# Last outputs in halves of heads with the gate behind them, a second search level on rounded 16-bit places, and another order of the first turn of x

## The chip, the cores and the metric

The kernel runs on one core of one Trainium2 chip. The metric is the time of one execution on the device in microseconds (us). Its engines are PE (TensorE; PEld is its weight load), DVE (VectorE), ACT (ScalarE), POOL (GpSimd, which issues the gathers and scatters) and SP (SyncE, which issues plain transfers).

## What is computed

A retention layer gives x, and a mixture of eight experts is applied to it. B=4, H=8, S=768, D=64; N=3072 tokens, DM=512, E=8 experts with F=1024, and a capacity of N/E=384 tokens each.

```
for t in range(S):
    state = gamma * state + einsum('bhd,bhe->bhde', k[:, :, t], v[:, :, t])
    y[:, :, t] = scale * einsum('bhd,bhde->bhe', q[:, :, t], state)
x = y.transpose(0, 2, 1, 3).reshape(N, DM)
logits = x @ w_gate                                  # [N, E]
for idx in argsort(-logits.flatten()):               # greedy, best first
    tok, e = idx // E, idx % E
    if assigned[tok] < 0 and counts[e] < N // E:
        assigned[tok] = e; counts[e] += 1
for e in range(E):
    out[assigned == e] = relu(x[assigned == e] @ w1[e]) @ w2[e]
```

Every product with a weight is made of three: a number is split into a high part (w1h, w2h, xh, hh) and a rest (w1l, w2l, xlo, hl), and high by high, high by rest and rest by high are summed.

## The kernel before

**Retention.** The 4 batches by 6 chunks of 128 tokens are 24 units, in 14 groups of one or two. For a group, `scores` makes masked scores (am, on DVE), `outputs` starts y from the state (T by queries, into the PSUM tile yp), `mix` adds the values by am and ACT copies yp to ys, and `states` goes on. `gate(c)` multiplies ys of chunk c by the gate's weights (32 matmuls), ACT copies the logits (gs), and PE transposes them. Behind the last group come eight `by_two` matmuls over the chunks that are already known, the last gate, the transpose, and four more `by_two`. The rows of x that are left are transposed in between (xr) and written to DRAM (xs) by SP.

**Search.** For each expert in turn the threshold of its 384 best tokens is sought in levels of 64 candidates: `cmp` compares the 24 tokens of each of the 128 partitions with 64 thresholds th (128x1536 results, in two instructions), PE counts them (x12 matmuls), DVE negates half of the counts (ng) and makes of them which expert is full (sg), PE adds over partitions, and DVE takes the place of the step (nmb). The second level takes its 64 thresholds inside the step that was found. Then come the threshold tv, the full expert's code, the chosen tokens Wq, their running places (Sc, s) and, by a one-hot of the places (A, V, ob), the token numbers idx, by which POOL gathers x (xg). bad, et, oix, eo and lim close an expert, and m, oh, eqc, a open the next. The first expert's search stands alone; the others stand between the experts' matmuls.

**Turn and experts.** A gathered tile of 128 tokens is transposed by PE (`turn_x`, L1029, pt), copied by ACT (xh, L1034) and subtracted by DVE (xlo). Three tiles make an expert's 384 tokens. Then `mm1` runs f0 to f7, twelve products each (L1079), ACT takes the positive part (hh) and DVE its rest (hl), and `mm2` runs three tiles of 24 products (L1121), whose results ACT copies (yo) and POOL scatters. For the first expert `by_thirds` (L1058) makes the products of w1h by xh of f0 and f1 as each third of x comes in, so that `mm1` has only the products with w1l and with xlo left for these two; `HOT` (23) and `WAIT` (3) are matmuls on zeros that fill PE's time ahead of the first tile and behind the first turn.

**Order.** Each engine runs its instructions in the order in which the code issues them. For the experts a planner in the code does this: it adds up a clock for PE, DVE, POOL and DMA (DVE by the number of elements of each counted instruction), and after each three products decides whether a step of the next search (`side.tick`), a split of weights, a gather or a turn is issued (`feed.tick`). What an expert needs and isn't issued when it begins is issued there at once (`force`). All counted DVE instructions carry the line of a helper: L162 before, L165 after.

Of the kernel before, what the change touches and what calls it, by code (L numbers as in the profile page):

```python
# [56 lines left out]
WAIT = 3  # L57
THIRDS = 2
FILL = (5, 7)
READY0 = 0  # L60
BITS = (6, 6, 5, 5, 5, 5)
# [4 lines left out]
def tile_retention_moe(ctx: ExitStack, tc: tile.TileContext, qkv, wg, w1, w2,  # L66
# [26 lines left out]
    near = sw.tile([128, 4], F32, name="near")  # L93
    top = sw.tile([128, 1], F32, name="top")
    gridn = [sw.tile([128, 64], F32, name=f"gridn{i}") for i in range(2)]
# [21 lines left out]
    def constants():  # L117
# [6 lines left out]
        nc.gpsimd.iota(iot, pattern=[[1, 64]], base=0, channel_multiplier=0, allow_small_or_imprecise_dtypes=True)  # L124
        for t, k in ((iolow, 1), (iohigh, 32)):
            nc.gpsimd.iota(t, pattern=[[k, t.shape[1]], [0, t.shape[2]]], base=0, channel_multiplier=0,
                           allow_small_or_imprecise_dtypes=True)
# [109 lines left out]
    def span_parts(pool, psum):  # L237
# [19 lines left out]
        def grids():  # L257
# [8 lines left out]
            for i, f in enumerate((WINDOW / 64, WINDOW / 4096, -WINDOW, -WINDOW * 65 / 64)):  # L266
                nc.vector.tensor_scalar(near[:, i:i + 1], step, float(f), None, op0=OP.mult)
            for i in range(2):
                nc.vector.tensor_scalar(gridn[i], iot, near[:, i:i + 1], near[:, i + 2:i + 3], op0=OP.mult, op1=OP.add)
# [7 lines left out]
    offn, qn = {}, {}  # L277
# [120 lines left out]
    def outputs(us):  # L398

        c = units[us[0]][1]  # L400
        for u in us:
            yps[u] = rp.tile([128, HP, C], F32, name="yp", bufs=2)
        if c:
            for pr in range(HP):
                for u in us:
                    b = units[u][0]
                    for s in range(2):
                        o = 64 * (s ^ b % 2)
                        nc.tensor.matmul(yps[u][o:o + 64, pr, :], T[b // 2][64 * s:64 * s + 64, b % 2, pr, :],  # L409
                                         st[u][1][64 * s:64 * s + 64, pr, :], start=(pr == 0), stop=False,  # L410
                                         skip_group_check=True)
# [4 lines left out]
    def mix(us):  # L416

        c = units[us[0]][1]
        for u in us:
            b, yp = units[u][0], yps.pop(u)  # L420
            for pr in range(HP):
                for s in range(2):
                    o = 64 * (s ^ b % 2)
# [993 lines left out]
```

## Time and profile before

| | |
|---|---|
| time, median of 3 runs | 403.05 us (403.01 to 403.31) |
| profiled execution | 400.03 us, its span 398.3 us |
| PE busy | 387.9 us, 97% of the span |
| DVE, ACT, POOL busy | 68%, 39%, 37% |
| retention ends, first search | 82.5 to 97.9 us |
| first turn of x | 102.2 to 110.4 us |
| PE's last matmul ends | 392.9 us |

The profile is of one execution. A row of the timeline is: start, duration, engine, line, operation, out<-in, partitions x elements and type, count, and in brackets how long the engine was idle before it and what ended that. Instructions that stand together are one row with a count. Behind PE's last matmul come the last copies and the last scatter, up to 398.3.

### The profile page before, as it was taken

The page shows a single profiled execution, that of the slowest core. Times are in us where ns is not written, and L with a number is a line of the kernel's source. Part 1 is how long each engine was busy: PE and PEld are TensorE (multiplying, and loading weights), DVE is VectorE, ACT ScalarE, POOL GpSimd, SP SyncE. Part 2 cuts the span into 40 slices and gives each one's busy share as a digit, 9 for nine tenths or more (in the row PEclk, how much of TensorE's full clock was granted, in tenths as well). Part 3 has the DMA queues.
Part 4 walks back from the last instruction along what each step waited for, and adds up shares of the span by engine and source line. Part 5 has one row for each costly group of instructions (what it writes and reads, how often), then busy time and mean ns, then how long its engine had stood idle before and what let it go on. Part 6 is the DMA issues. An engine that isn't in the chain of part 4 may idle for free.

```text
span 398.3 us, 8481 instructions
## 1 busy us (share of the span) xinstructions
PE 387.9 (97%) x3460; PEld 338.6 (85%) x3462; DVE 269.9 (68%) x641; ACT 156.4 (39%) x285; POOL 148.0 (37%) x165
## 2 busy tenths in 40 slices
PE   8999999998999999999999999999999999999994
PEld 6988989974798889879988987898799889889983
DVE  6459868967998589858868885887687157156300
ACT  1422424243471265147325524343454165156210
POOL 6488783202520720361262341353265138021011
PEclk9999999999999999999999999999999999999999
DMA  7999988987653671483365482366147316710001
GB/s 291 423 414 420 408 312 259 227 209 257 198 199 105 183 256 54 143 289 135 107 212 238 149 294 112 95 221 241 54 160 251 144 53 183 318 54 26 2 27 59
DMA packets 22824, 77.50 MB, mean 195 GB/s; under 512 B 2677, under 2 KB 11639, under 8 KB 16121
## 3 DMA queue, kind: packets, MB, share of 16 engines
q0 software_dynamic: 8448, 46.14, 33.0%
q1 hardware_dynamic: 14330, 30.74, 21.5%
q8 instruction: 29, 0.48, 0.5%
q14 instruction: 17, 0.14, 0.1%
HBM read 64.29 MB, written 12.58 MB: 193 GB/s over the span
## 4 chain that ended last, share of the span: by engine, by line
PE 68%; issue 13%; DVE 7%; DMA 7%; POOL 2%; ACT 1%; POOLq 1%; SPq 0%; another core or an unknown queue 0%; DVEq 0%; ACTq 0%
PE py L1121 25%; PE ph L1079 24%; DMA ld<-qkv 5%; PE yp L424 4%; PE sc L377 3%; PE pt L1029 2%; PE psm L162 2%; PE yp L409 2%; DVE am L380 2%; PE sc L514 1%; PE TP L439 1%; DVE cmp L162 1%; DMA out<-yo,oix 1%; POOL wraw L983 1%; DMA xg<-xs,idx 1%
## 5 line engine op out<-in xcount | busy, mean ns | idle before, releaser
L1079 PE MATMUL ph<-xh,w1h 128*128 128x384 f32 x248 | 81.8, 343 | 0.0
L1079 PE MATMUL ph<-xlo,w1h 128*128 128x384 f32 x256 | 81.7, 335 | 0.0
L1079 PE MATMUL ph<-xh,w1l 128*128 128x384 f32 x256 | 81.5, 335 | 0.0
L1121 PE MATMUL py<-w2h,hh 128*128 128x512 f32 x184 | 75.2, 409 | 0.0
L1121 PE MATMUL py<-w2l,hh 128*128 128x512 f32 x184 | 72.1, 392 | 0.0
L1121 PE MATMUL py<-w2h,hl 128*128 128x512 f32 x184 | 72.1, 392 | 0.0
L1102 POOL DMA_INDIRECT out<-yo,oix x23 | 27.9, 1215 | 106.1 <-ACT yo L1099 99.4
L983 POOL DMA_INDIRECT wraw<-w,wix x32 | 38.5, 1203 | 60.8 <-DVE un L162 47.0
L1084 ACT ACTIVATE hh<-ph 128x384 fp32r<-128x384 f32 x64 | 31.4, 490 | 62.0 <-PE ph L1079 61.3
L162 DVE TENSOR_TENSOR w1l<-wraw,w1h 128x1024 fp32r<-128x1024 f32 (+1 forms) x36 | 39.2, 1101 | 14.2 <-ACT w1h L1002 14.2
L1079 PEld LDWEIGHTS ph<-xlo,w1h 128*128 128x128 f32 x256 | 47.7, 188 | 0.0
L1079 PEld LDWEIGHTS ph<-xh,w1l 128*128 128x128 f32 x256 | 47.7, 188 | 0.0
L1079 PEld LDWEIGHTS ph<-xh,w1h 128*128 128x128 f32 x248 | 46.4, 188 | 1.1 <-ACT xh L1034 0.4
L162 DVE SCALAR_TENSOR_TENSOR hl<-ph,hh 128x384 fp32r<-128x384 f32 x64 | 34.8, 553 | 18.2 <-ACT hh L1084 17.7
L1016 POOL DMA_INDIRECT xg<-xs,idx x24 | 28.7, 1196 | 41.3 <-issue 30.9
L380 DVE TENSOR_TENSOR am<-sc,dm 128x512 f32<-128x512 f32 x48 | 30.0, 683 | 18.4 <-PE sc L377 18.4
L1121 PEld LDWEIGHTS py<-w2h,hl 128*128 128x128 f32 x184 | 34.5, 188 | 7.4
L162 DVE TENSOR_TENSOR w2l<-wraw,w2h 128x1024 fp32r<-128x1024 f32 x32 | 38.6, 1219 | 2.3 <-ACT w2h L1002 2.3
L1121 PEld LDWEIGHTS py<-w2l,hh 128*128 128x128 f32 x184 | 34.7, 189 | 6.2 <-DVE w2l L162 0.6
L1121 PEld LDWEIGHTS py<-w2h,hh 128*128 128x128 f32 x184 | 34.7, 188 | 5.6
L1099 ACT ACTIVATE yo<-py 128x512 f32<-128x512 f32 x23 | 13.7, 597 | 58.6 <-PE py L1121 43.3
L1002 ACT ACTIVATE w1h<-wraw 128x1024 fp32r<-128x1024 f32 (+1 forms) x36 | 33.6, 957 | 4.7 <-DMA wraw<-w,wix 4.7
(189 smaller groups left out, 556.0 us busy)
## 6 DMA issues: line engine op xcount, KB each, us to landing
ld<-qkv SPq DMA_DIRECT2D x20, 1024.0 KB, 11.9
xs<-x SPq DMA_DIRECT2D x32, 128.0 KB, 3.4
ld<-qkv SPq DMA_DIRECT2D x4, 768.0 KB, 5.3
xs<-xr SPq DMA_DIRECT2D x7, 256.0 KB, 2.2
wraw<-w,wix POOLq DMA_INDIRECT x32, 7.3
xg<-xs,idx POOLq DMA_INDIRECT x24, 3.7
out<-yo,oix POOLq DMA_INDIRECT x23, 3.1
xs<-x SPq DMA_DIRECT2D x4, 64.0 KB, 1.8
```

Of the source, the lines that this page charges most:

```text
L162: return f(o, *a, **k)
L377: nc.tensor.matmul(sc[s][:, pr, :], k_[r, w], q_[r, w], start=True, stop=True)
L380: masked.append(nc.vector.tensor_tensor(am[:, s], sc[s], dm[:, s], op=OP.mult))
L424: nc.tensor.matmul(yp[o:o + 64, pr, :], values(u)[:, 2 * pr + s, :], st[u][0][:, s, pr, :], start=(not c and pr == 0), stop=(pr == HP - 1) ...
L983: nc.gpsimd.indirect_dma_start(out=t, out_offset=None, in_=w1v if nm == "w1" else w2v, in_offset=bass.IndirectOffsetOnAxis(ap=wix[:, hf:hf ...
L1002: nc.scalar.activation(p[0], p[2], AF.Copy)
L1016: nc.gpsimd.indirect_dma_start(out=t, out_offset=None, in_=xs, in_offset=bass.IndirectOffsetOnAxis(ap=found[n][0][:, j:j + 1], axis=0))
L1079: nc.tensor.matmul(ph, a[:, o:o + 128], x_[:, d], start=(k == 0 and not begun), stop=(k == len(prods) - 1), skip_group_check=begun)
L1084: nc.scalar.activation(hh[:, f], ph, AF.Relu)
L1099: nc.scalar.activation(yo, py, AF.Copy)
L1102: sct = nc.gpsimd.indirect_dma_start(out=out, out_offset=bass.IndirectOffsetOnAxis(ap=oix[:, j:j + 1], axis=0), in_=yo, in_offset=None, bo ...
L1121: nc.tensor.matmul(py, h_[:, f, t], a[:, o:o + DM], start=(k == 0), stop=(k == 23))
```

## The change

1. In the last group (`halved`) `outputs` and `mix` work in two halves of the heads, each in a PSUM bank of its own, and ACT copies four halves of 128x256. `gate(NC - 1)` stands directly behind the loop; the eight early `by_two` come behind it and end their sum, ng is taken from it at once, and the last two chunks are counted in eight matmuls of 64x8.
2. In the second level of the search the 64 thresholds are no longer compared. From the step's start (`starts`, `at`, two columns) each token's place in the grid, x, is worked out, rounded to a whole number in 16 bits (`place`, four copies) and compared with the numbers 0 to 63 (`ramp`). `off`, `qn`, `q` and `sel` go; tv comes first, `ge` is new.
3. In the first turn of x one filling matmul stands behind the first turn (`WAIT`), the second turn comes next, then both thirds of the first tile, and so on; the search's step stands ahead of the rest of the weights and of xlo.

```diff
-WAIT = 3
+WAIT = 1
...
+NEAREST = 12582912.0
...
     def below(n, tv):
         th = sw.tile([128, 64], F32, name="th")
-        ve.tensor_scalar(th, gridn[0], tv, None, op0=OP.add)
+        ve.tensor_scalar(th, gridn, tv, None, op0=OP.add)
         yield th
-        offn[n] = sw.tile([128, 64], F32, name="off")
-        ve.tensor_scalar(offn[n], gridn[1], tv, None, op0=OP.add)
-        qn[n] = sw.tile([128, 1], F32, name="qn")
-        ve.tensor_scalar(qn[n], gridn[1][:, 0:1], tv, near[:, 1:2], op0=OP.add, op1=OP.subtract)
+        starts[n] = sw.tile([128, 2], F32, name="starts")
+        ve.tensor_scalar(starts[n], near[:, 3:5], tv, None, op0=OP.add)
         yield
+
+    def places_in_grid(m, at):
+        x = sw.tile([128, COLS], F32, name="x")
+        ve.tensor_scalar(x, m, at, near[:, 5:6], op0=OP.subtract, op1=OP.mult)
+        place = sw.tile([128, COLS, 4], BF, name="place")
+        ve.tensor_scalar(place, bc(x, 4), NEAREST, -NEAREST, op0=OP.add, op1=OP.add)
+        return place
+
+    def reach_place(cols, place, cmp):
+        p_ = place[:, cols]
+        k = p_.shape[1]
+        tt(cmp[:, cols].rearrange("p c (j r) -> p c j r", r=4), p_[:, :, None, :].to_broadcast([128, k, 16, 4]),
+           ramp.rearrange("p (j r) -> p j r", r=4)[:, None].to_broadcast([128, k, 16, 4]), OP.is_ge)
...
-            for u in us:
-                mix([u])
-                states([u])
+            if g == len(groups) - 1:
+                mix(us)
+            else:
+                for u in us:
+                    mix([u])
+                    states([u])
...
+        gate(NC - 1)
         pc = rp.tile([128, 2 * E], F32, name="sc", bufs=4)
...
-            by_two(pc, cmp0, oh0, c, k == 0, False)
+            by_two(pc, cmp0, oh0, c, k == 0, k == len(early) - 1)
...
-        gate(c)
-        next(rows)
         lt = rp.tile([128, 512], F32, name="sc", bufs=4)
         nc.tensor.transpose(lt[:, 0:128], gs[c % 2], ident)
+        n0 = other_half(pc, nc.vector)
...
-        for b in range(B):
-            by_two(pc, cmp0, oh0, b * NC + NC - 2, False, b == B - 1)
-        n0 = other_half(pc, nc.vector)
+        for k in (NC - 2, c):
+            for b in range(B):
+                te.matmul(pc[0:64, 0:E], cmp0[:, b * NC + k, :], oh0[:, b * NC + k, :], start=False, stop=True,
+                          skip_group_check=True)
...
                 if not i:
-                    th = sw.tile([128, 64], F32, name="th")
-                    ve.scalar_tensor_tensor(th, nm.to_broadcast([128, 64]), near[:, 0:1], offn[n], op0=OP.mult,
+                    at = sw.tile([128, 2], F32, name="at", bufs=2)
+                    ve.scalar_tensor_tensor(at, nm.to_broadcast([128, 2]), near[:, 0:1], starts[n], op0=OP.mult,
                                             op1=OP.add)
                     cmp = sw.tile([128, COLS, 64], BF, name="cmp", bufs=2)
+                    place = places_in_grid(m, at[:, 1:2])
                     for h in range(2):
-                        cc = slice(h * COLS // 2, (h + 1) * COLS // 2)
-                        reach(cc, COLS // 2, m, cmp, th)
+                        reach_place(slice(h * COLS // 2, (h + 1) * COLS // 2), place, cmp)
                         if not h and n:
                             yield
-                    q = sw.tile([128, 1], F32, name="q", bufs=2)
-                    ve.scalar_tensor_tensor(q, nm, near[:, 0:1], qn[n], op0=OP.mult, op1=OP.add)
                 else:
+                    tv = sw.tile([128, 1], F32, name="tv", bufs=2)
+                    ve.scalar_tensor_tensor(tv, nm, near[:, 2:3], at[:, 0:1], op0=OP.mult, op1=OP.add)
                     eh = sw.tile([128, E], BF, name="eh")
                     ve.scalar_tensor_tensor(eh, num, nm, codet, op0=OP.is_equal, op1=OP.mult)
-                    tv = sw.tile([128, 1], F32, name="tv", bufs=2)
-                    ve.scalar_tensor_tensor(tv, nm, near[:, 1:2], q, op0=OP.mult, op1=OP.add)
+                    ge = sw.tile([128, COLS], BF, name="ge")
+                    ve.tensor_scalar(ge, m, tv, None, op0=OP.is_ge)
                     ve.tensor_reduce(code, eh, axis=AX.X, op=OP.max)
-            sel = sw.tile([128, COLS], BF, name="sel")
-            ve.tensor_scalar(sel, a, code, None, op0=OP.is_equal)
-            ve.scalar_tensor_tensor(Wq[:, 0:COLS], m, tv, sel, op0=OP.is_ge, op1=OP.mult)
+            ve.scalar_tensor_tensor(Wq[:, 0:COLS], a, code, ge, op0=OP.is_equal, op1=OP.mult)
...
     lows = []
+    turn_x(0, 0, lows)
+    fill(WAIT)
     for j in range(KT):
-        if j == 1:
-            by_thirds(0, range(1))
-        turn_x(0, j, lows)
-        if not j:
-            fill(WAIT)
-        if j:
-            side.step()
-            by_thirds(j - 1, range(1 if j == 1 else 0, THIRDS))
-        if j < KT - 1:
+        if j + 1 < KT:
+            turn_x(0, j + 1, lows)
+        by_thirds(j, range(THIRDS))
+        side.step()
+        if j + 1 < KT:
             low_w(quarters[j])
         lows.pop(0)[1]()
-    by_thirds(KT - 1, range(THIRDS))
-    side.step()
```

The order on DVE in the first turn of x, before. w1l is the rest of the weights of f0 and f1, xlo that of x, ng and sg belong to the first level's counts of expert 1:

```order
L162 TENSOR_TENSOR cmp<-m,th 128x768
L162 TENSOR_TENSOR w1l_1802<-wraw_98,w1h_1801 128x512
L162 TENSOR_TENSOR xlo<-pt,xh 128x4x128
L162 TENSOR_SCALAR ng<-psm 64x8
L162 TENSOR_TENSOR w1l_1802<-wraw_98,w1h_1801 128x512
L162 TENSOR_TENSOR xlo<-pt,xh 128x4x128
L162 SCALAR_TENSOR_TENSOR sg_93<-psm,ng 64x8
L162 TENSOR_TENSOR xlo<-py,xh 128x2x128 x2
L162 TENSOR_REDUCE nmb<-psm 128x1
L162 SCALAR_TENSOR_TENSOR th<-nmb,near,off 128x64
L162 TENSOR_TENSOR cmp<-m,th 128x768
```

The same stretch after:

```order
L165 TENSOR_SCALAR ng<-psm 64x8
L165 TENSOR_TENSOR w1l_1810<-wraw_98,w1h_1809 128x512
L165 TENSOR_TENSOR xlo<-pt,xh 128x4x128
L165 SCALAR_TENSOR_TENSOR sg_93<-psm,ng 64x8
L165 TENSOR_TENSOR w1l_1810<-wraw_98,w1h_1809 128x512
L165 TENSOR_TENSOR xlo<-pt,xh 128x4x128
L165 TENSOR_REDUCE nmb<-psm 128x1
L165 SCALAR_TENSOR_TENSOR at<-nmb,near,starts 128x2
L165 TENSOR_SCALAR x<-m,at,near 128x24
L165 TENSOR_SCALAR place<-x 128x96
L165 TENSOR_TENSOR cmp<-place,ramp 128x768
L165 TENSOR_TENSOR xlo<-py,xh 128x2x128 x2
```

ng went from behind the first xlo to ahead of the first w1l, and the last xlo (x2) from ahead of nmb to behind the comparison.

DVE around the first part of w2l of expert 0 (two instructions for one half of the weights), before: un ends the search of expert 1, s to bad number its tokens.

```order
L162 TENSOR_TENSOR un<-un,Wq 128x24
L162 TENSOR_TENSOR w2l_1971<-wraw,w2h_1970 128x1024 x2
L162 SCALAR_TENSOR_TENSOR hl<-ph,hh 128x384
L162 SCALAR_TENSOR_TENSOR s_2035<-psm,Wq 128x24
L162 SCALAR_TENSOR_TENSOR bad<-psm,bad 128x1
```

The end of the same block after:

```order
L165 SCALAR_TENSOR_TENSOR bad<-both,code,bad 128x1
L165 TENSOR_REDUCE et<-oh 128x1
L165 TENSOR_REDUCE et<-un 128x1
L165 SCALAR_TENSOR_TENSOR bad<-et,bad 128x1
L165 SCALAR_TENSOR_TENSOR hl<-ph,hh 128x384 x2
L165 TENSOR_TENSOR w2l_1995<-wraw,w2h_1994 128x1024
L165 TENSOR_TENSOR w2l_2048<-wraw,w2h_2047 128x1024 x2
```

One of the two stays ahead of s; the second stands behind the block and two hl, directly ahead of the other half of the weights.

PE at the third turn of expert 1 (pt), where mm2 of expert 0 (py) ends and f0 of expert 1 (ph) begins, before:

```order
L1029 MATMUL pt<-ident,xg 128x128 x4
L1121 MATMUL py<-w2h_2013,hh 128x512
L1121 MATMUL py<-w2l_2014,hh 128x512
L1121 MATMUL py<-w2h_2013,hl 128x512
L1121 MATMUL py<-w2h_2013,hh 128x512
L1121 MATMUL py<-w2l_2014,hh 128x512
L1121 MATMUL py<-w2h_2013,hl 128x512
L1079 MATMUL ph<-xh,w1h_2229 128x384 x3
```

And after:

```order
L1056 MATMUL pt<-ident,xg 128x128 x4
L1148 MATMUL py<-w2h_2047,hh 128x512
L1148 MATMUL py<-w2l_2048,hh 128x512
L1148 MATMUL py<-w2h_2047,hl 128x512
L1056 MATMUL pt<-ident,xg 128x128 x4
L1106 MATMUL ph<-xh,w1h_2216 128x384 x3
```

No product of mm2 stands between the turn and the first product with xh any more. At expert 3 the third turn also stands directly ahead of the first product.

## Rows read from the trace of the kernel before

**Rows 1.** The page: busy us, share of the span and instructions of each engine.

```profile
PE 387.9 (97%) x3460; PEld 338.6 (85%) x3462; DVE 269.9 (68%) x641; ACT 156.4 (39%) x285; POOL 148.0 (37%) x165
```

**Rows 2.** Stretches: us, busy PE PEld DVE ACT POOL, clock, DMA share, GB/s.

```profile
82.50:97.90 15.40, 12.81 (x152) 8.82 (x150) 10.65 (x48) 6.11 (x15) 1.26 (x3) 1.00 0.79 228
107.60:393.00 285.40, 284.98 (x1649) 251.75 (x1648) 189.76 (x441) 119.02 (x191) 91.11 (x97) 1.00 0.43 152
```

**Rows 3.** Timeline of PEld: the first turn of x.

```profile
102.21 0.42 PEld L1029 LDWEIGHTS pt<-ident,xg 128*128 128x128 f32 x4 [0.56 <-DMA xg<-xs,idx]
```

**Rows 4.** Timeline, end of the retention and last gate.

```profile
84.69 0.36 PE L162 MATMUL sc<-oh,cmp 128*128 128x16 bf16 x8
85.25 1.27 PE L514 MATMUL sc<-ys,wgf 128*32 128x128 f32 x32
86.62 0.28 ACT L516 ACTIVATE gs<-sc 128x128 f32<-128x128 f32 x1 [1.21 <-PE sc L514]
```

**Rows 5.** Timeline of DVE, first expert's search.

```profile
88.41 0.17 DVE L230 TENSOR_SCALAR ng<-sc 64x8 f32<-64x8 f32 x1 [0.34 <-PE sc L162]
89.09 0.15 DVE L162 TENSOR_REDUCE nmb<-psm 128x1 f32<-128x8 f32 x1
89.59 1.83 DVE L162 TENSOR_TENSOR cmp<-m,th 128x768 bf16<-128x768 f32 x2
93.17 0.23 DVE L162 TENSOR_SCALAR sel<-a,code 128x24 bf16<-128x24 bf16 x1
```

**Rows 6.** Timeline of DVE, a comparison of 16-bit operands.

```profile
121.91 0.62 DVE L162 TENSOR_TENSOR ob<-low,iolow 128x384 bf16<-128x384 int16 x2
```

**Rows 7.** Timeline of DVE, turn stage.

```profile
103.66 0.68 DVE L162 TENSOR_TENSOR w1l<-wraw,w1h 128x512 fp32r<-128x512 f32 x1
104.27 0.68 DVE L162 TENSOR_TENSOR xlo<-pt,xh 128x512 fp32r<-128x512 f32 x1
105.05 0.17 DVE L162 TENSOR_SCALAR ng<-psm 64x8 f32<-64x8 f32 x1
106.70 0.76 DVE L162 TENSOR_TENSOR xlo<-py,xh 128x256 fp32r<-128x256 f32 x2
107.78 0.17 DVE L162 TENSOR_REDUCE nmb<-psm 128x1 f32<-128x8 f32 x1 [0.33 <-PE psm L162]
108.30 0.96 DVE L162 TENSOR_TENSOR cmp<-m,th 128x768 bf16<-128x768 f32 x1
```

**Rows 8.** Timeline of PEld, turn stage.

```profile
103.60 0.52 PEld L1058 LDWEIGHTS ph<-xh,w1h 128*128 128x128 f32 x4 [0.58 <-ACT xh L1034]
108.20 0.71 PEld L1079 LDWEIGHTS ph<-xlo,w1h 128*128 128x128 f32 x4
```

**Rows 9.** Timeline, expert 0's last f, next search, and its mm2.

```profile
116.25 0.16 DVE L162 TENSOR_REDUCE nmb<-psm 128x1 f32<-128x8 f32 x1
117.78 2.35 DVE L162 TENSOR_TENSOR w2l<-wraw,w2h 128x1024 fp32r<-128x1024 f32 x2
120.52 0.17 DVE L162 SCALAR_TENSOR_TENSOR s<-psm,Wq 128x24 int16<-128x24 f32 x1
123.05 0.22 DVE L162 SCALAR_TENSOR_TENSOR bad<-et,bad 128x1 f32<-128x1 f32 x1
121.62 0.33 PE L1079 MATMUL ph<-xh,w1h 128*128 128x384 f32 x1
123.70 0.39 PE L1121 MATMUL py<-w2h,hh 128*128 128x512 f32 x1
125.32 0.40 PE L1121 MATMUL py<-w2l,hh 128*128 128x512 f32 x1
```

**Rows 10.** Timeline, a later turn of x and the first f0 behind it.

```profile
178.11 0.60 PE L1029 MATMUL pt<-ident,xg 128*128 128x128 f32 x4
178.74 0.60 ACT L1034 ACTIVATE xh<-pt 128x512 fp32r<-128x512 f32 x1 [2.34 <-PE pt L1029]
179.39 0.98 PE L1079 MATMUL ph<-xh,w1h 128*128 128x384 f32 x4
```

More of the change, by code (lines that the diff above doesn't have):

```diff
@@ L92, in tile_retention_moe @@
     grid = sw.tile([128, 64], F32, name="grid")
-    near = sw.tile([128, 4], F32, name="near")
+    near = sw.tile([128, 6], F32, name="near")
+    gridn = sw.tile([128, 64], F32, name="gridn")
+    ramp = sw.tile([128, 64], BF, name="ramp")
     top = sw.tile([128, 1], F32, name="top")
-    gridn = [sw.tile([128, 64], F32, name=f"gridn{i}") for i in range(2)]
     Wq = sw.tile([128, COLS + 1], BF, name="Wq")
@@ L265, in grids @@
             nc.vector.scalar_tensor_tensor(top, step, float(ABOVE - 1), bd[:, 1:2], op0=OP.mult, op1=OP.subtract)
-            for i, f in enumerate((WINDOW / 64, WINDOW / 4096, -WINDOW, -WINDOW * 65 / 64)):
+            first = -WINDOW * 65 / 64
+            for i, f in enumerate((WINDOW / 64, -WINDOW, WINDOW / 4096, first - WINDOW / 4096, first + WINDOW / 8192)):
                 nc.vector.tensor_scalar(near[:, i:i + 1], step, float(f), None, op0=OP.mult)
-            for i in range(2):
-                nc.vector.tensor_scalar(gridn[i], iot, near[:, i:i + 1], near[:, i + 2:i + 3], op0=OP.mult, op1=OP.add)
+            nc.vector.reciprocal(near[:, 5:6], near[:, 2:3])
+            nc.vector.tensor_scalar(gridn, iot, near[:, 0:1], near[:, 1:2], op0=OP.mult, op1=OP.add)
         return over_tokens, over_partitions, grids
@@ L418, in mix @@
         c = units[us[0]][1]
+        halved = us[-1] == nu - 1
         for u in us:
[L420 to L423, printed above, removed]
-                    nc.tensor.matmul(yp[o:o + 64, pr, :], values(u)[:, 2 * pr + s, :], st[u][0][:, s, pr, :],
-                                     start=(not c and pr == 0), stop=(pr == HP - 1), skip_group_check=True)
+            b = units[u][0]
             YS[b, c] = (yk.tile([128, HP, C], F32, name=f"ys{b}_{c}") if b + B * c >= TURNED else
                         yk.tile([128, HP, C], F32, name="ys", bufs=9))
-            nc.scalar.activation(YS[b, c], yp, AF.Copy)
+        for p in ((0, 2), (2, HP)) if halved else ((0, HP),):
+            for u in us:
+                b, yp = units[u][0], yps[u][p[0] // 2]
+                for pr in range(*p):
+                    for s in range(2):
+                        o = 64 * (s ^ b % 2)
+                        nc.tensor.matmul(yp[o:o + 64, pr, :], values(u)[:, 2 * pr + s, :], st[u][0][:, s, pr, :],
+                                         start=(not c and pr == 0), stop=(pr == p[1] - 1), skip_group_check=True)
+                nc.scalar.activation(YS[b, c][:, p[0]:p[1]], yp[:, p[0]:p[1]], AF.Copy)
+        for u in us:
+            yps.pop(u)
     def states(us):
@@ L651, in tile_retention_moe @@
         f()
-        next(rows)
-        next(rows)
-        for b in range(B):
-            by_two(pc, cmp0, oh0, b * NC + NC - 2, False, b == B - 1)
-        n0 = other_half(pc, nc.vector)
+        for _ in range(3):
+            next(rows)
+        for k in (NC - 2, c):
+            for b in range(B):
+                te.matmul(pc[0:64, 0:E], cmp0[:, b * NC + k, :], oh0[:, b * NC + k, :], start=False, stop=True,
+                          skip_group_check=True)
         full(pc, n0, sgs[0])
```

14 lines of the change are left out of this document (9 added, 5 removed).

## The prediction

> **What bounds the kernel now.** I read first the busy shares of the page: PE works 97% of the span [rows 1]. Then the table by stretches [rows 2]: from 107.6 us to the end of PE's work at 393 us PE is busy in 284.98 of 285.40 us, DVE in 189.76 and ACT in 119.02; the granted clock is 1.00 in each stretch. So behind the first expert's turn of x the kernel is one queue of matmuls with no slack: what starts it earlier or later moves the end by as much, and a new wait of PE in it is paid in full. The only stretch with much PE idle time is 82.5 to 97.9, where PE is busy in 12.81 of 15.40 us: the end of the retention, the last gate and the first expert's search, one chain through PE, ACT and DVE. From there the chain goes through the first gather of x, whose landing PE waits for at 102.21 [rows 3], and into the turn stage, 102.2 to 110.4. So the change has three places where it can act directly (last gate, search, turn stage), and a fourth: the planner counts DVE's elements, so other element counts move weight splits, turns and searches of the later experts.
>
> **1. Last gate ahead of the early counts.** Before, the eight early counts stand from 84.69 in front of the gate's 32 matmuls, which begin at 85.25; the gate takes 1.27 us, and the copy gs starts at 86.62 [rows 4]. After, the copies are halves, and the gate stands directly behind mix. I take 0.56 (84.69 to 85.25) plus a little of the gate's own waiting, 0.60 earlier. Bounds: 0.36, if only the counts' busy time goes, and 0.8. The eight counts then stand between gate and transpose, while ACT copies gs (0.28 us), and hide there in good part; if they don't, they eat some of the gain, which the lower bound holds.
>
> **2. The negation ng ahead.** It stood between the last counts and sg, 88.41 with 0.17 us [rows 5]; it now runs early. The four last counts become eight small ones, about 0.1 us more. Together 0.1 earlier; bounds 0 and 0.2.
>
> **3. Second level of the search.** Before: nmb 89.09, th, then two comparisons of 1.83 us together from 89.59 to 91.42, so 2.33 us [rows 5]. After: nmb, at, x, place, and two comparisons with both operands in 16 bits. The nearest row of that kind is ob, two of 128x384 in 0.62 us from 16-bit operands in the same order of four [rows 6]; twice the elements would be 1.24 us, less one fixed part per instruction, so about 1.02. From nmb to the comparison I count four short steps of 0.2 to 0.3 us, 1.07 in place of 0.50. The sum is 2.09, 0.24 earlier; bounds 0.4 earlier and, were the comparison no faster than before, 0.55 later. At the end of the search sel goes from behind code [rows 5], but ge and tv stand in the same short chain: 0.1 earlier, bounds 0 and 0.25.
>
> Together the index, the gather and the 23 filling matmuls move by 0.60 + 0.10 + 0.24 + 0.10 = **1.04 us earlier** (0.4 to 1.5), and the landing of x with them.
>
> **4. The turn stage.** PE's own list gets shorter: two fills fewer. But PE goes over to the products with xlo of all three turns, and there DVE decides. Before, DVE used the time in which it waited for PE's counts: w1l 103.66, xlo 104.27, and only then ng at 105.05; the last turn's two halves of xlo came at 106.70, took 0.76 and were done before nmb at 107.78; PE's loads of xlo at 108.20 followed without a wait [rows 7, 8]. After, ng stands in front of w1l and of the first xlo. PE's counts stand behind both first thirds now: these wait for xh until 103.60 [rows 8], as before, and with eight matmuls for four the counts end again at about 105.0. So DVE stands idle from about 103.5 to 105.1, and the 1.3 us of w1l and xlo come behind. And nmb, at, x, place and one comparison stand in front of the last xlo. With the steps of [rows 7] (w1l 0.61 from start to start, xlo of the same size likewise) and 0.1 for sg: ng 105.1, w1l 105.2, xlo 105.8, sg 106.45, w1l 106.55, xlo 107.2, nmb 107.8, then 1.07 to the comparison at 108.9, 0.48 for it, the two halves of xlo at 109.35 and 109.75. PE has by then done its four wlo products and waits; it starts the first xlo product at about 109.85 and not at 108.20: **1.65 later**, all seen from the landing. Bounds 1.2 (short steps at 0.13 each) and 2.1 (comparison at its old price). If nothing of this happened, PE would gain the two fills, 0.4.
>
> **5. Expert 0's second products.** Before, both halves of w2l's first part run at 117.78 to 120.13, ahead of the block s to bad (120.52 to 123.27), and PE's mm2 from 123.70 on, with the first product that needs the second half at 125.32, never waits for them [rows 9]. After, the second half stands behind s to bad and behind the last two hl. I count from the end of f4 on PE: hl of f4 starts 0.55 later (ACT hh between), the end of the next search takes 1.53 (116.25 to 117.78), hl of f5 0.47, the first half of w2l 1.16, then s waits for PE until about 4.4, the block takes 2.66, two hl 1.0, the second half 1.2: done at 9.3. PE needs it after three more f of 2.08 each (121.62 to 123.70 is one), two small matmuls and 1.62 us of mm2 (123.70 to 125.32), at 8.0. So **1.25 later**; bounds 0.6 and 1.6. It adds to the former term, since hl of f4 waits for PE and not for DVE.
>
> **6. Turns of experts 1 and 3.** A turn before shows the latency: transposes at 178.11, copy xh 178.74 to 179.34, first product f0 at 179.39 [rows 10]; three products of mm2, 0.9 us from 178.46 on, fill the time. In the new order the third turn of experts 1 and 3 is followed at once by f0, which reads all of xh. PE then waits what those three filled: **0.85 each, 1.7** together; bounds 0.5 and 1.0 each (at expert 1 the copy yo stands in front of xh on ACT too). Expert 1's second weights are also gathered one scatter later on POOL; the slack there looked near zero, so 0 to 0.6, taken as 0.1. Against it stands a wait of 0.3 us for a comparison in expert 1, in the 0.42 us of idle that the last long stretch has [rows 2], which the shorter comparison should remove: -0.3.
>
> **Sum.** -1.04 + 1.65 + 1.25 + 1.7 + 0.1 - 0.3 = +3.36 us. The profiled execution is 400.03 us (span 398.3); it becomes 403.4. The runs' median, 403.05, lies 3.02 above the profiled one, so the forecast is 406.4. With its bounds the case reaches from 404.7 to 407.9: the bounds do not all fall on one side.
>
> **Rivals.**
> *A, faster.* DVE is never late: the planner or my count of DVE's order has slack that I overlook (for instance the comparison takes less than 0.4 us, and PE reaches f0 later than I think), and the turns find other work in front of f0. Then the earlier landing, 1.04, the fills, 0.4, and the wait of 0.3 reach the end: 403.05 - 1.74 = 401.3. For it: before, PE waited nearly nowhere in 285 us [rows 2], so the order has been slack so far. Against it: terms 4 and 5 name the instructions that stand in front, and term 6 a latency that a row shows. It decides at term 4: xlo of the last turn must be done within 1.65 us of the time that I give.
> *B, no change.* Only the turn stage's wait appears and the rest hides: -1.04 + 1.65 - 0.3 = +0.3, 403.4.
> *C, slower still.* PE stands for some 1.8 us in term 4, longer than at any place behind 20.6 us before. If the granted clock then falls to 1.2 GHz, the 16 products of f0 and f1, 0.17 us each, would take 2.8 us more: 409.2. For it speaks only that the wait is new; every stretch of before shows 1.00 [rows 2]. The Trainium skill, "TensorE: Matmul & The Clock Gate", section "What's actually happening", says that an idle TensorE is set to 1.2 GHz. By that rule this rival is possible; no row of before shows such a fall, and the sum would be 2.8 us more.
> *D, the comparison is not faster* with rounded 16-bit places, since the values that are compared are read with repeats. The row of ob [rows 6], with repeats of the same kind, speaks against it. It would add 0.8 in the search and 0.4 in term 4: 407.6.
>
> **How the numbers follow.** The forecast's case (waits in at least two of terms 4 to 6) with D gets 0.60, C 0.04, B 0.16, A 0.20. The predicted time is that of the likeliest, 406.4. Its own range is 404.7 to 407.9; to leave out no more than 2 in 10 the range goes down to 402.4, which takes in B and what lies between, and leaves out A and C. A measurement can tell about 0.2%, 0.8 us, from no change. Slower by more, the forecast's case and C: 0.64; within, B: 0.16; faster, A: 0.20.
>
> **What would show it.** In the profile after: gs at about 86.0, PE's first turn at about 101.2 (terms 1 to 3). PE idle for about 1.8 us in front of the loads of xlo by f0, ended by DVE xlo, with nmb, at, x, place and cmp in front of it on DVE (4). An idle time of about 1.2 us in mm2 of expert 0, ended by DVE w2l (5). Two idle times of about 0.85 us ended by ACT xh in front of f0 (6). Wrong would be: the landing not earlier, PE without waits behind 108, or a granted clock under 1.00.

## The result

The changed kernel takes 406.15 us (median of 6, 404.51 to 407.74) against 402.95 (median of 6, 402.28 to 403.31): ratio 1.0078, 95% interval 1.0054 to 1.0102, so 3.2 us slower. Its profiled execution took 405.33 us, span 403.6. One thing has to be known to read the numbers below: the kernel before ran near 400 us on one of the three chips of the experiments (medians 399.92 and 400.33) and near 403 on the two others (403.49 and 402.60), and its profiled execution (400.03) lies with the former; so each experiment below stands beside the runs of before that were made with it.

PE stays the bound, but it now waits. The page after has, in the groups of lines, three rows in which PE was idle (the end of a row: the idle time before these instructions, and what ended most of it); before, each of these groups had 0.0:

```profile
PE 388.3 (96%) x3462; PEld 338.5 (84%) x3464; DVE 265.1 (66%) x642; ACT 157.5 (39%) x287; POOL 141.6 (35%) x166
...
L1106 PE MATMUL ph<-xh,w1h 128*128 128x384 f32 x248 | 81.9, 344 | 2.1 <-ACT xh L1061 2.1
...
L1106 PE MATMUL ph<-xlo,w1h 128*128 128x384 f32 x256 | 81.6, 336 | 1.8 <-DVE xlo L165 1.8
...
L1148 PE MATMUL py<-w2l,hh 128*128 128x512 f32 x184 | 72.3, 393 | 2.1 <-DVE w2l L165 1.5
```

The table by stretches (us, then busy us of PE, PEld, DVE, ACT, POOL, then the granted clock) answers to [rows 2]. PE idles 1.76 us in the three us around the first xlo products, and 4.1 us behind them, where before it had 0.42:

```profile
106.00:109.00 3.00, 1.24 (x9) 0.92 (x9) 2.86 (x9) 0.90 (x2) 2.10 (x2) 1.00 0.51 134
...
109.00:393.00 284.00, 279.86 (x1621) 246.71 (x1622) 185.09 (x438) 118.43 (x188) 81.59 (x94) 1.00 0.43 151
```

**Gate and search came as counted.** The timeline of the last two gates: the gate of the chunk before stands at 81.01, the last gate at 85.22, its copy gs at 86.50. In the profile before, the gate of the chunk before stood at 80.49 (first row), so this execution's retention ran 0.52 late ahead of all that was changed:

```profile
80.49 1.08 PE L514 MATMUL sc<-ys,wgf 128*32 128x128 f32 x32
```

```profile
81.01 1.08 PE L539 MATMUL sc<-ys,wgf 128*32 128x128 f32 x32
...
85.22 1.18 PE L539 MATMUL sc<-ys,wgf 128*32 128x128 f32 x32
...
86.50 0.28 ACT L541 ACTIVATE gs<-sc 128x128 f32<-128x128 f32 x1 [0.77 <-PE sc L539]
```

From the one gate to gs it was 6.13 us (to 86.62, [rows 4]) and is 5.49. In the search, nmb 88.77 to the end of the two comparisons 90.90 is 2.13 us, where it was 2.33 [rows 5]:

```profile
88.77 0.16 DVE L165 TENSOR_REDUCE nmb<-psm 128x1 f32<-128x8 f32 x1
...
89.87 1.03 DVE L165 TENSOR_TENSOR cmp<-place,ramp 128x768 bf16<-128x768 bf16 x2
```

The first transposes of x (their weight loads) start at 101.09, and not at 102.21 [rows 3]:

```profile
101.09 0.58 PEld L1056 LDWEIGHTS pt<-ident,xg 128*128 128x128 f32 x4
```

Counted from the gate of the chunk before, that is 20.08 us and not 21.72. Of the 1.64, gate, negation and search give 1.2; the other 0.45 lies between idx and the transposes (4.34 us, before 4.79), where nothing was changed.

**The turn stage.** DVE's timeline shows the order of the change in time: ng waits 1.23 us for PE's counts, w1l and xlo stand behind it, and nmb to cmp stand ahead of the last xlo. PE's load of xlo ends a wait of 2.08 us (1.76 of PE itself) [rows 7, 8]:

```profile
104.09 0.17 DVE L165 TENSOR_SCALAR ng<-psm 64x8 f32<-64x8 f32 x1 [1.23 <-PE psm L165]
...
104.30 0.69 DVE L165 TENSOR_TENSOR w1l<-wraw,w1h 128x512 fp32r<-128x512 f32 x1
...
105.02 0.69 DVE L165 TENSOR_TENSOR xlo<-pt,xh 128x512 fp32r<-128x512 f32 x1
...
106.90 0.15 DVE L165 TENSOR_REDUCE nmb<-psm 128x1 f32<-128x8 f32 x1
...
107.91 0.56 DVE L165 TENSOR_TENSOR cmp<-place,ramp 128x768 bf16<-128x768 bf16 x1
...
108.39 0.75 DVE L165 TENSOR_TENSOR xlo<-py,xh 128x256 fp32r<-128x256 f32 x2
```

```profile
108.86 0.65 PEld L1106 LDWEIGHTS ph<-xlo,w1h 128*128 128x128 f32 x4 [2.08 <-DVE xlo L165]
```

**Expert 0's w2l** [rows 9]. The second half starts at 126.08, behind the block that ends with bad and behind two hl; PE's product that needs it starts at 127.34:

```profile
125.01 0.22 DVE L165 SCALAR_TENSOR_TENSOR bad<-et,bad 128x1 f32<-128x1 f32 x1
...
126.08 2.35 DVE L165 TENSOR_TENSOR w2l<-wraw,w2h 128x1024 fp32r<-128x1024 f32 x2
...
127.34 0.50 PE L1148 MATMUL py<-w2l,hh 128*128 128x512 f32 x1 [1.11 <-DVE w2l L165]
```

**Turns** [rows 10]. At expert 1 the copy of the third turn waits on ACT behind the copy yo, and f0 waits for it:

```profile
144.10 0.60 PE L1056 MATMUL pt<-ident,xg 128*128 128x128 f32 x4
...
144.35 0.60 ACT L1126 ACTIVATE yo<-py 128x512 f32<-128x512 f32 x1
...
144.84 0.59 ACT L1061 ACTIVATE xh<-pt 128x512 fp32r<-128x512 f32 x1
...
145.48 0.79 PE L1106 MATMUL ph<-xh,w1h 128*128 128x384 f32 x3 [0.79 <-ACT xh L1061]
```

At expert 3 the same, 0.76 us at 220.30, with yo and ng in front of xh. Three more waits, which the prediction did not have, stand at experts 2, 3 and 4; at expert 2 (182) the copies xh of the second and third turn run one behind the other, the second turn's 2.6 us behind the modelled end of its transposes (178.82):

```profile
181.42 1.08 ACT L1061 ACTIVATE xh<-pt 128x512 fp32r<-128x512 f32 x2 [2.23 <-PE pt L1056]
...
182.56 0.80 PE L1106 MATMUL ph<-xh,w1h 128*128 128x384 f32 x3 [0.53 <-ACT xh L1061]
...
241.71 0.50 PE L1148 MATMUL py<-w2l,hh 128*128 128x512 f32 x1 [0.60 <-issue]
...
280.01 0.50 PE L1148 MATMUL py<-w2l,hh 128*128 128x512 f32 x1 [0.35 <-DVE w2l L165]
```

The idle time that the profile gives is less than the loss, as a product's modelled end lies 0.16 us behind the start of the next one (a product of 512 columns is given 0.39 us, and the next starts 0.23 us after it). By starts, the product at 127.34 comes 1.50 us after the one ahead of it and not 0.23, so 1.27 is lost; the others lose about 1.0 (145), 0.7 (182), 1.0 (220), 0.75 (241) and 0.5 (280).

### The profile page after: what moved, and what is told of

It is laid out like the page before. It is cut to its first block, busy times and chain, and to the rows that moved or that the text cites. A ratio compares the mean times of both kernels' runs of the same rounds, so it can differ in the third digit from the quotient of the medians.

```text
span 403.6 us, 8492 instructions
## 1 busy us (share of the span) xinstructions
PE 388.3 (96%) x3462; PEld 338.5 (84%) x3464; DVE 265.1 (66%) x642; ACT 157.5 (39%) x287; POOL 141.6 (35%) x166
## 5 line engine op out<-in xcount | busy, mean ns | idle before, releaser
L1129 POOL DMA_INDIRECT out<-yo,oix x23 | 26.2, 1138 | 95.5 <-ACT yo L1126 84.1
L1010 POOL DMA_INDIRECT wraw<-w,wix x32 | 34.6, 1083 | 68.6 <-DVE un L165 58.8
L1043 POOL DMA_INDIRECT xg<-xs,idx x24 | 27.8, 1156 | 55.0 <-issue 33.9
```

What stands on the lines that cost most here:

```text
L1010: nc.gpsimd.indirect_dma_start(out=t, out_offset=None, in_=w1v if nm == "w1" else w2v, in_offset=bass.IndirectOffsetOnAxis(ap=wix[:, hf:hf ...
L1043: nc.gpsimd.indirect_dma_start(out=t, out_offset=None, in_=xs, in_offset=bass.IndirectOffsetOnAxis(ap=found[n][0][:, j:j + 1], axis=0))
L1129: sct = nc.gpsimd.indirect_dma_start(out=out, out_offset=bass.IndirectOffsetOnAxis(ap=oix[:, j:j + 1], axis=0), in_=yo, in_offset=None, bo ...
```

## Experiments

All kernels below are made of the kernels before and after. The ratio given with each result is the record's own estimate and not the quotient of the two medians; it lies up to 0.003 from it. "Held" means that the planner adds the element counts of the old search and gets, at the end of the first turn, the clocks that it has in the kernel before. PE's order is then that of before behind f1 of expert 0, and the direct effect of an edit can be told from that of the planner's moves (a kernel that is only "fed" gets the counts, and not the clocks):

```diff
         ve.tensor_scalar(starts[n], near[:, 3:5], tv, None, op0=OP.add)
+        clk.dve += (151 + 64 + 151 + 1 - 151 - 2) / 0.96
...
                     place = places_in_grid(m, at[:, 1:2])
+                    clk.dve += (151 + 64 - 3 * 151 - 2 - 24 - 96) / 0.96
...
+                    clk.dve += (151 + 1) / 0.96
                 else:
...
+    clk.pe, clk.dve, clk.pool, clk.dma = 21615.625, 24906.667, 24115.625, 29391.625
+    clk.busy[:] = [(21615.625, 22865.625), (22865.625, 24115.625)]
+    side.due = 23725.417
+    arrive.update({("w1", 1, 0): 21946.75, ("w2", 0, 0): 27678.625, ("w2", 1, 0): 30591.625})
     for n in range(E):
         feed.expert(n)
```

### Each part by itself

**Part 1 alone** (the diff of the change in outputs, mix, the end of the loop, and the counts). Expected:

> The kernel before with part 1 alone (last outputs in halves, gate behind them, ng ahead); the planner's order is that of before. Theory (direct edits help a little, the new orders cost): gs at 86.0 to 86.5 and the first transpose of x 0.1 to 0.6 us earlier, no new wait of PE behind 108, time 0.1 to 0.7 us under before. Rival (the halves themselves delay the retention's end, by the 0.5 us that the last group stands later in the profile after): landing not earlier, time 0 to 0.5 us over before.

Measured: 402.08 us (10 runs) beside 403.49 (25 runs of before), ratio 0.9984, interval 0.9958 to 1.0011: by the time alone not told from no change. The trace tells it: from the gate of the chunk before to gs 5.48 us (6.13 before), and from gs to idx 10.60 (10.80 before, ng). So the rival falls: the retention's end is not delayed by the halves. The late retention of the profile after is a matter of the execution: over the traces of this study the gate of the chunk before starts anywhere from 79.9 to 82.9, whatever was changed behind it. "No new wait of PE" did not hold; the wait that came is shown under parts 1 and 2.

**Part 2 alone**, planner fed the old counts, old turn. Expected:

> The kernel before with part 2 alone, and the planner's DVE clock fed the element counts of the old search, so that all engines keep the order of before. Theory: the new search is quicker by itself: second level 0.2 to 0.4 us shorter in the first search, the wait of 0.27 us for a comparison at 149 gone, time 0.3 to 0.9 us under before. Rival (the comparison or the roundings cost more than they save): second level not shorter, time equal or over before.

Measured: 402.74 us beside 403.49, ratio 0.9995, interval 0.9970 to 1.0021. From gs to idx 10.45 us and not 10.80, and the wait for a comparison at 149 is gone. The gain is there, 0.35 us in the first search, at the lower end of what was expected; the time cannot show it.

**Parts 1 and 2**, planner fed, old turn. Expected:

> Parts 1 and 2 together with the turn of x of before, planner fed the old counts, so the order of before everywhere behind the first search. Theory: the gains add and nothing is lost behind them: PE idle behind 108 under 0.5 us, time 0.7 to 1.5 us under before. Rival (an earlier landing is eaten by DVE, which is the bound of the turn stage anyway): PE waits in the turn stage and time within 0.3 us of before.

Measured: 401.98 us beside 403.49, ratio 0.9975, interval 0.9946 to 1.0005. By the time alone, not told from no change. In the trace gs comes 5.49 us behind the gate ahead, idx 10.26 behind gs, so 1.2 us earlier in all, and PE reaches the xlo products 0.27 us earlier still: the gains add. But the expected "idle under 0.5 us" failed: in this trace, as in those of parts 1 and 2 alone, PE stands 1.9 to 2.0 us near 207, which the profile before does not show, though the order is the same. The timeline of part 1 alone shows it: PE's counts end at 205.91, ACT's ng starts only at 208.60, and PE's sum (psm) waits for sg. Behind it the products of mm2 start 0.43 us apart and not 0.23:

```profile
205.45 0.46 PE L162 MATMUL psm<-oh,cmp 128*128 128x16 bf16 x12
...
206.43 0.95 POOL L996 DMA_INDIRECT wraw<-w,wix  x1 [0.30 <-issue]
...
208.60 0.17 ACT L228 ACTIVATE ng<-psm 64x8 f32<-64x8 f32 x1 [5.03 <-PE py L1134]
...
209.02 0.17 PE L162 MATMUL psm<-sg,onesb 128*128 128x8 bf16 x1 [1.92 <-DVE sg L162]
...
210.31 0.63 PE L1134 MATMUL py<-w2h,hl 128*128 128x512 f32 x1
...
210.73 0.63 PE L1134 MATMUL py<-w2h,hh 128*128 128x512 f32 x1
```

The table by stretches of the same kernel gives the granted clock: 1.00 while PE stands, then its lower level, 0.50 (1.2 GHz), and 1.00 again from 213 on:

```profile
208.00:209.00 1.00, 0.00 (x0) 0.00 (x0) 0.16 (x1) 0.38 (x2) 0.00 (x0) 1.00 0.94 377
...
211.00:212.00 1.00, 1.00 (x3) 0.72 (x3) 1.00 (x3) 0.25 (x1) 0.00 (x0) 0.50 1.01 426
...
213.00:214.00 1.00, 1.00 (x7) 0.78 (x6) 1.00 (x1) 0.60 (x1) 0.00 (x0) 1.00 0.93 393
```

About eight products of 0.43 us cost 1.6 us more than at 1.00. The mean granted clock of the timed runs suggests that the fall comes in about half of the executions: of the ten runs of e3_gate_search (parts 1 and 2), five have 0.994 or 0.995 and took 402.5 to 403.6, five have 0.998 or 0.999 and took 400.6 to 401.5. In the profile before the same ng started at 206.23, 0.09 us behind the counts:

```profile
205.68 0.46 PE L162 MATMUL psm<-oh,cmp 128*128 128x16 bf16 x12
...
206.23 0.17 ACT L228 ACTIVATE ng<-psm 64x8 f32<-64x8 f32 x1 [2.42 <-PE psm L162]
```

**Part 3 alone** (order of the first turn and one fill), planner free. Expected:

> The kernel before with part 3 alone (order of the first turn, one fill); the planner moves what it moves by it. Theory: DVE decides there: PE stands 1.2 to 2 us in front of f0's products with xlo (the old comparison of 0.87 us stands ahead of it), and at expert 1, where the third turn again stands directly ahead of f0, 0.7 to 0.9 us; time 1.5 to 3 us over before. Rival (the new order of the turn gains its two fills and the waits are made by the new search): no such waits, time 0.2 to 0.5 us under before.

Measured: 411.41 us beside 403.49, ratio 1.0222, interval 1.0189 to 1.0254: 7.9 us slower by the medians. PE's timeline has the wait in front of xlo, one for w2l of expert 0, and two at the turn of expert 1:

```profile
111.30 0.96 PE L1079 MATMUL ph<-xlo,w1h 128*128 128x384 f32 x4 [1.64 <-DVE xlo L162]
...
130.23 0.50 PE L1121 MATMUL py<-w2l,hh 128*128 128x512 f32 x1 [1.54 <-DVE w2l L162]
...
148.26 0.66 PE L1029 MATMUL pt<-ident,xg 128*128 128x128 f32 x4 [1.01 <-DVE xlo L162]
...
149.61 1.32 PE L1079 MATMUL ph<-xh,w1h 128*128 128x384 f32 x4 [0.69 <-ACT xh L1034]
```

Behind the last two the clock fell to 0.50 (150 to 152), and the late uptake was there too (1.93 us near 216). The mechanism is the one expected; the size, 1.5 to 3 us, was too small by the clock and by w2l, which was not in the expectation. The rival falls.

### Direct effect or planner's moves

**All three parts, held.** Expected:

> All three edits of the change, but the planner is fed the old element counts and its clocks are set, at the end of the first turn, to what they are in the kernel before: behind f1 of expert 0 every engine has the order of before. Theory (two losses: DVE in the turn stage, and the planner's moves): PE stands 1.6 to 1.9 us in front of f0's products with xlo as in the profile after; the waits of after at 126, 145, 182, 220, 241 and 280 are gone; the wait of 1.95 us for sg near 207, which the three kernels with the order of before showed, is there. From the landing 1.0 earlier and 1.75 of wait, 0.3 to 1.0 us over before, up to 2.5 if the granted clock falls behind the wait too. Rival (the planner's moves cost nothing by themselves, all of it comes from the turn's wait): as the changed kernel, 2.5 to 3.5 us over before.

Measured: 401.39 us beside 399.92, ratio 1.0031, interval 1.0015 to 1.0047: 1.5 us slower. Here before ran near 400, and the wait near 207, which was expected too, is not in this trace. PE has one wait of over 0.5 us behind 97 us, 1.75, where it was expected, and behind it the clock fell in the profiled execution:

```profile
108.29 0.97 PE L1109 MATMUL ph<-xlo,w1h 128*128 128x384 f32 x4 [1.75 <-DVE xlo L165]
```

```profile
111.00:112.00 1.00, 1.00 (x5) 1.00 (x4) 0.00 (x0) 0.19 (x1) 0.00 (x0) 0.50 0.97 410
```

In the profile after the same wait (1.76) was not followed by a fall. The waits at 126, 145, 182, 220, 241 and 280 are gone with the planner's moves. The theory of two losses holds: the rival wanted 2.5 to 3.5 us.

**Parts 1 and 2, old turn, planner free**, to be set beside the held order. Expected:

> Parts 1 and 2 with the turn of before, planner fed the new element counts, so the later experts' orders move: beside e3_gate_search the planner's moves alone. Theory: the third turn of expert 2 stands directly ahead of its f0 and costs 0.7 to 0.9 us there, and other waits of 0.3 to 1.2 us for w2l or sg show; time 0.5 to 3 us over e3_gate_search, unless the wait near 207 falls away with the new order, which would give back up to 3.5. Rival (planner's moves are harmless): PE idle behind 108 as in e3_gate_search, time within 0.4 us of it.

Measured: 403.58 us beside 399.92, ratio 1.0086, interval 1.0062 to 1.0109. The kernel with the same parts and the old order (e7_ng_on_dve below; it differs besides by ng alone, which did nothing to the kernel before on this chip) took 398.46 in the same series: the planner's moves cost 5.1 us by themselves, more than the 0.5 to 3 expected. PE's timeline:

```profile
179.10 0.98 PE L1106 MATMUL ph<-xh,w1h 128*128 128x384 f32 x4 [1.07 <-ACT xh L1061]
...
218.36 0.80 PE L1106 MATMUL ph<-xlo,w1h 128*128 128x384 f32 x3 [0.74 <-DVE xlo L165]
...
240.23 0.50 PE L1148 MATMUL py<-w2l,hh 128*128 128x512 f32 x1 [1.13 <-DVE w2l L165]
...
275.38 0.50 PE L1148 MATMUL py<-w2l,hh 128*128 128x512 f32 x1 [0.69 <-DVE w2l L165]
```

The turn in front of f0, at expert 2 here, costs 1.07 by itself. All of these are waits for ACT or DVE; that the planner's clock takes these instructions for done in time is argued, not measured.

**The turn stage with xlo ahead of the step**, all else as in the held kernel:

```diff
         by_thirds(j, range(THIRDS))
-        side.step()
         if j + 1 < KT:
             low_w(quarters[j])
         lows.pop(0)[1]()
+        side.step()
```

Expected:

> As e5_all_held, but in the turn stage each step of the search stands behind the weights' rest and xlo of that turn on DVE, not ahead of them. Theory: xlo of the last turn then comes some 1.3 us earlier and ng no longer holds up the first; PE's wait in front of f0's xlo products falls under 0.5 us, and what is left is the gain of gate and search and the two fills: 1.0 to 1.8 us under before. Rival (DVE has too much work in the stage whatever the order): the wait stays over 1 us or comes back at the comparison or the counts of f2 and f3, time within 0.5 us of before.

Measured: 398.85 us beside 399.92, ratio 0.9973, interval 0.9955 to 0.9991. DVE's timeline has w1l ahead of ng again, and the last xlo ahead of nmb, and PE does not wait for it:

```profile
103.20 0.69 DVE L165 TENSOR_TENSOR w1l<-wraw,w1h 128x512 fp32r<-128x512 f32 x1
...
104.89 0.17 DVE L165 TENSOR_SCALAR ng<-psm 64x8 f32<-64x8 f32 x1 [0.40 <-PE psm L165]
...
106.36 0.74 DVE L165 TENSOR_TENSOR xlo<-py,xh 128x256 fp32r<-128x256 f32 x2
...
107.15 0.17 DVE L165 TENSOR_REDUCE nmb<-psm 128x1 f32<-128x8 f32 x1
```

From PE's first transposes to its first xlo product it takes 5.83 us, before 6.16, after 7.55 and with all parts held 7.67. So the new order of PE is good for 0.3 us; what cost 1.8 was the place of the search's step on DVE.

### The late uptake

**Parts 1 and 2, planner fed, old turn, and ng of experts 2 to 7 on DVE:**

```diff
-                    pc, ng = count_pairs(cmp, oh, None if n > 1 else ve)
+                    pc, ng = count_pairs(cmp, oh, nc.vector if n > 1 else ve)
```

Expected:

> As e3_gate_search, and the negation ng of experts 2 to 7 runs on DVE and not on ACT, not counted by the planner, so no order moves. Theory (ACT took up PE's counts 2.7 us late near 206, PE stood 1.95 us for it and its clock fell to 0.50 for some 3 us behind): wait and fall are gone, granted clock 1.00 from 110 to 393, time 2.5 to 4 us under e3_gate_search, near 398.5. Rival (the late count is late for each engine while POOL issues gathers): DVE takes it up late too, PE stands there 1.5 to 2 us, and the time is that of e3_gate_search, 402.

Measured: 398.46 us beside 399.92, ratio 0.9978, interval 0.9961 to 0.9995, and no wait near 207. That says nothing on ACT or DVE: before ran near 400 in this series, and no trace from this chip has the wait. The time shows parts 1 and 2 once more, 1.5 us by the medians and 0.2 to 1.6 by the interval. So the edit was put alone into the kernel before, twice:

> The kernel before with ng of experts 2 to 7 on DVE in place of ACT, nothing else. Theory (the late uptake is ACT's): where before shows the wait near 207 this kernel has none and is 2.5 to 4 us under it; where before has no such wait the two are equal within 0.5 us. Rival (each engine takes the count up late there): the same wait, ended by DVE ng, and the same time as before.

> e11_before_ng once more, in case before shows its slow form this time (median near 403.5, with the late uptake of the count near 206). Theory (the late uptake is ACT's): this kernel then has no wait near 207, granted clock 1.00 behind it, and is 2.5 to 4 us under before. Rival (each engine takes the count up late there): the wait is there, ended by DVE ng, and the times are equal. If before runs near 400 again, the two are equal within 0.5 us and the question stays open.

Measured first: 400.26 us beside 400.33, ratio 1.0002, interval 0.9991 to 1.0013, no late uptake anywhere: open. Then, on another chip: 403.60 beside 402.60, ratio 1.0006, interval 0.9975 to 1.0037, and the wait is there, now ended by DVE:

```profile
206.20 0.46 PE L162 MATMUL psm<-oh,cmp 128*128 128x16 bf16 x12
...
207.19 0.95 POOL L983 DMA_INDIRECT wraw<-w,wix  x1 [0.30 <-issue]
...
209.37 0.17 DVE L230 TENSOR_SCALAR ng<-psm 64x8 f32<-64x8 f32 x1 [4.84 <-PE py L1121]
...
209.78 0.18 PE L162 MATMUL psm<-sg,onesb 128*128 128x8 bf16 x1 [1.94 <-DVE sg L162]
```

The counts end at 206.66, ng starts 2.7 us later, as on ACT. My theory fell: it is not ACT. In both traces the count ends while POOL issues a gather, and ng starts 1.2 us behind the end of POOL's next one (207.38 to 208.60, and 208.14 to 209.37); but in the profile before POOL issued at the same places and ng started at once.

It is not DVE either: the count is not taken up late, PE reports it late. An engine tells the others by a semaphore that it is done, and the traces hold the time of each such signal. In e1_gate PE's signal of the count comes at 208.53, 2.62 us behind the modelled end, together with those of the next two groups of matmuls, 0.05 to 0.06 us apart, and ng starts 0.07 us behind it; in e12_before_ng it comes at 209.34, 2.68 behind the end. The three other traces with the wait (e2_search, e3_gate_search, e4_turn) show the same, 2.63 to 2.68 us. In the profile before the signal came 0.02 us behind the end. DVE, ACT and POOL have no late signal in any of these traces, as far as their signals are recorded. All five traces with the wait come from chips 0 and 14; in the seven from chip 7 no signal of PE in the mixture is late. Whether PE's work or only its signal was held up the trace does not tell, since the ends are modelled, and what makes the difference between chips stays open.

### The changed kernel again, and a better one

Expected of the changed kernel beside before once more:

> The changed kernel itself again, beside the kernel before on the same chip. Theory (its losses are its own waits, 5.9 us of PE idle behind 106 in its profile; before has or has not the wait near 207 depending on the chip): where before runs near 403.5 the changed kernel is 2.5 to 3.5 us over it, where before runs near 400 it is 4.5 to 6 over it; PE idles in the same seven places, and the granted clock falls behind one of them in some executions. Rival (the difference is a fixed 0.8 per cent): 3.2 us over before in either case.

Measured: 405.91 us beside 400.33, ratio 1.0146, interval 1.0126 to 1.0167: 5.6 us slower where before has no late uptake. The same waits are there but the one at 182. At that place the order is that of the profile after, and xh started 0.04 us behind the modelled end of its transposes; in the profile after PE's signals of the second and third turn came at 181.40 and 181.53, the second turn's so over 2.5 us late. So the wait at 182 is of the kind near 207, and not the planner's. The rival of a fixed ratio falls.

The held kernel with xlo ahead of the step, and ng on DVE:

> e6_xlo_first with ng of experts 2 to 7 on DVE as in e7_ng_on_dve: gate and search of the change, the turn with xlo ahead of the search's step, the order of before everywhere else. Theory (the gains add): PE idle under 0.6 us behind 102, 1.0 to 1.8 us under before where before runs near 400, 3.5 to 5 where it runs near 403.5. Rival (ng on DVE delays other work there, or the late uptake moves to DVE): no better than e6_xlo_first.

Measured: 398.27 us beside 400.33, ratio 0.9944, interval 0.9927 to 0.9960: 2.1 us under before (1.0 to 1.8 expected), and better than both kernels. Behind 97 us its profile has no idle time of PE over 0.25 us. What it gains over e6_xlo_first (0.6 us, each beside its own runs of before) is within the intervals, so the rival, no better than e6_xlo_first, is not excluded.

## Why the prediction was right, and where not

The time, 406.4 forecast and 406.15 measured, and the direction are right, and so are the places of the losses that it names. That the number is so close is luck: two errors of about 2 us cancelled. The sum was 3.36 and the profiled executions differ by 5.3; the step from profile to median was 3.02 for before and is 0.82 after (405.33 to 406.15).

- **Terms 1 to 3** (1.04 us earlier): right. gs 0.65 (forecast 0.60), ng 0.2 (0.10), search 0.35 (0.24 and 0.10); 1.2 together, the same in each trace with parts 1 and 2. The two 16-bit comparisons took 1.03 us (1.02), and nmb to the comparison 1.10 (1.07). Rival D falls. That the first transposes stood at 101.09, where the forecast had 101.2, is luck in part: 0.45 us between idx and the transposes, which no term had, made good for most of the 0.52 by which this retention ran late; over the traces that stretch took 4.34 to 5.36 us.
- **Term 4** (+1.65): right. ng came at 104.09, the last xlo at 108.39 and PE's first xlo product at 108.86; the forecast's chain, 1.04 earlier, gives 104.06, 108.31 and 108.81. Held apart from all else it was the 1.75 us wait of e5_all_held, and it went when the step went behind xlo. (The 108.20 of before, which the forecast calls a product's start, is the load of its weights.)
- **Term 5** (+1.25): right, 1.27 by starts.
- **Term 6** (0.85 each): right in place, too small: 1.0 each. At expert 1 yo, and at expert 3 ng, stood on ACT in front of xh; I had seen yo and put it into the bound alone. The wait of 0.3 us for a comparison is gone, as forecast.
- **The 0.1 for what else the planner moves** is the term that was mis-sized: waits for w2l at experts 3 and 4 lose 0.75 and 0.5. I had read the order of the later experts for turns alone, and not each split of w2l against the product that needs it. The 0.7 at the turn of expert 2 belongs to no term: it is PE's late signal, and e9_after_again did without it. With the measured sizes the sum is about 4.7 us, and 5.4 with the late signal.
- **The step from profile to median** failed. I took the 3.02 us by which the timed runs of before lay above its profiled one as common to both kernels. Four traces with the order of before (e1_gate, e2_search, e3_gate_search, e12_before_ng) hold a wait of 1.92 to 1.98 us near 207 and about 1.6 us of lower clock behind it, which the profiled execution of before had not; 400.03 plus the wait is 402.0, plus both 403.6, and its timed runs, 402.28 to 403.31, lie between. The changed kernel's searches stand elsewhere, and neither of its traces has that wait. That the timed runs of before hold it is argued from these sister kernels; no execution of before that had it was traced. Where before runs near 400, the change costs 5.6 us.
- **Rival C** was half right: a wait of 1.75 to 1.98 us can be followed by the lower clock, for 1.6 us, and in some executions is not. I had priced it at 2.8 us and given it 4 in 100, and had named a granted clock under 1.00 as a sign of being wrong; it is 1.00 throughout the mixture in the profile after, but not, it seems, in the timed runs. Four of the six runs of after have a mean granted clock of 0.992 and took 405.9 to 407.7; the two of 0.996 and 0.997 took 404.5 and 405.3; no execution with 0.992 was traced. The Trainium skill, "TensorE: Matmul & The Clock Gate", section "What's actually happening", says that an idle TensorE is set to 1.2 GHz. The trace of e5_all_held agrees, 0.50 behind a wait of 1.75 us; that of the changed kernel does not, 1.00 behind 1.76.
- **The chances**: the range was to leave out no more than 2 in 10, but leaves out A and C, to which 0.24 was given.

## What to carry over

An edit that is priced by the instructions that it adds and removes can lose more by what it moves: here the direct edits gain 1.2 us, and a planner that counts elements turned that into 4 to 5 us of waits. Hold the order fixed when you try such an edit, and read a moved order instruction by instruction against the one that needs it. On an engine with a queue in order, put what the bound engine waits for ahead of a step that itself waits for that engine; and before a profile's time is carried over to a median, look in traces of sister kernels for a wait that comes and goes.

## What the runs showed of the hardware

- An idle time of PE of 1.92 us (e1_gate) and of 1.75 us (e5_all_held) was followed, within 1 us of its end, by some 3 us at a granted clock of 0.50; 1.76 us in the profile after and 1.74 us in e9_after_again were not. A fall cost about 1.6 us, nearly as much again as the wait.
- PE's signal of a count came 2.62 to 2.68 us behind the modelled end, together with those of the next two groups, in five traces from chips 0 and 14, and 0.02 us behind it in the profile before; DVE, ACT and POOL had none in the same traces, as far as their signals are recorded.
- Comparing 128x768 with both operands in 16 bits took 0.56 us for one, 1.03 for two, against 0.96 and 1.83 with 32-bit operands.
